# Putting every engine of an attention-plus-MLP kernel into hand-made program order, with a pipelined start and more PSUM banks for the first MLP group

## The chip, the cores and the metric

The kernel runs on one core of a Trainium2 chip. The metric is device time in microseconds of one launch, lower is better; beside it the text uses the span of one profiled launch. A launch takes 1.8 us more than its own span; the medians quoted are of other launches too. With one core there is no second die to compare; every run quoted here is of the fast state (within 1.5% of the fastest of its kernel), and every experiment is on record as correct.

Engine names in the profile: PE does matmuls, PEld loads their weights, DVE is the vector engine, ACT the scalar engine, POOL the GpSimd engine, SP issues most DMAs. SBUF is the on-chip memory; PSUM is the accumulator memory that PE writes; this kernel uses it as 8 banks, each of 128 partitions by 512 float32.

## The reference, cut to what matters

Two stages. First a causal linear attention with a decay per head, in blocks of 64 tokens with a carried state, then an MLP on the result (B=4, H=8, S=768, D=64; 3072 tokens, 512 to 2048 to 512):

```python
for b in range(nb):                      # blocks of 64 tokens, in order
    intra = einsum('bhic,bhjc->bhij', qb, kb) * Dmask
    intra = einsum('bhij,bhjd->bhid', intra, vb)
    inter = einsum('bhid,bhde->bhie', qb * lam_pow, kv_state)
    out[:, :, sl] = intra + inter
    kv_state = lam_block * kv_state + einsum('bhsd,bhse->bhde', kb * rev_pow, vb)
...
h = x @ w_in
s = sin(alpha * h)
g = h + s * s / (alpha + 1e-09)
return g @ w_out
```

## The kernel before

The attention is cut into 24 units (one batch, half of the heads, 256 tokens). Four units make a group of 512 tokens, which the MLP then takes. A unit goes through: scale q and k (into QL and KD) and cast v (into VB), eight transposes into PSUM, a copy of them to SBUF (QT), the score matmuls, a mask (ST), the output matmuls, and an update of the state. The MLP of a group has 16 blocks of `ffn1` (four matmuls of 128x512 into one PSUM bank, then sine on ACT, square on DVE or POOL, and `gall` on DVE, which reads the bank once more), and four tiles of `ffn2` (16 matmuls each, a copy to `ob` on ACT, a store).

The parts that matter (cuts marked with `...`):

```python
    RING = 10
    GATE = 9
    ...
    work = ctx.enter_context(tc.tile_pool(name="work", bufs=3))
    xtp = ctx.enter_context(tc.tile_pool(name="xt", bufs=3))
    outp = ctx.enter_context(tc.tile_pool(name="outp", bufs=3))     # ob
    ps = ctx.enter_context(tc.tile_pool(name="ps", bufs=1, space=PS))
    ...
    def transposes(u):                       # PSUM tag "s": one tile of two banks
        pt = ps.tile([P, 2, 2, 2, P], BF16, name="pt", tag="s", bufs=1)
        ...
    def scores(u):
        sp = ps.tile([P, 2, 2, 2, P], FP32, name="sp", tag="s", bufs=1)   # two banks
        ...                                  # 16 matmuls, then the mask in two halves
        for hd in range(2):
            nc.vector.tensor_tensor(out=ST[:, hd], in0=sp[:, hd], in1=mask..., op=ALU.mult)
    ...
    def ffn1(g, f, sq=None):
        hps = ps.tile([P, 512], FP32, name="hps", tag="hps", bufs=3)      # one bank
        ...                                  # 4 matmuls into hps
        def fin():
            nc.scalar.activation(out=s1[:], in_=hps[:], func=ACTF.Sin, scale=alpha_sb[:, f:f + 1])
            (sq or nc.vector).tensor_tensor(out=s2[:], in0=s1[:], in1=s1[:], op=ALU.mult)
            nc.vector.scalar_tensor_tensor(out=gall[g][:, f, :], in0=s2[:],
                                           scalar=r_sb[:, f:f + 1], in1=hps[:],
                                           op0=ALU.mult, op1=ALU.add)
        ...
    def ffn2(g, m):
        ops = ps.tile([P, DM], FP32, name="ops", tag="ops", bufs=1)
        ...                                  # 16 matmuls
        def fin():
            ob = outp.tile([P, DM], FP32, name="ob")
            nc.scalar.copy(out=ob[:], in_=ops[:])
            ...
            nc.sync.dma_start(out=out[r0:r0 + C, :].rearrange("(p two) d -> two p d", two=2),
                              in_=ob[:])
    ...
    with tc.manual_schedule(engines={ET.PE, ET.Pool, ET.SP}):
        ...                                  # units 0 to 3 one after the other
        for f in range(NFC):                 # first MLP group
            run(ffn1(0, f, nc.gpsimd if f % 2 else nc.vector))
            if f == GATE:                    # loads of units 4 to 13 wait for this block
                load(4, after=f1mm[0, f])
                for u in range(5, 4 + RING):
                    load(u)
        ...                                  # slots 4 to 27: a unit, and blocks of ffn1 and
                                             # ffn2 of earlier groups in between; ffn2(0) is
                                             # spread over slots 4 to 11
        for i in range(4):
            run(ffn2(NG - 1, i))             # the tail
```

PE, POOL and SP take their instructions in the order in which the program writes them; the order on ACT and DVE is left to the scheduler. The gate is the block of the first MLP group (`GATE`) whose last matmul releases the 30 loads of units 4 to 13. The eight PSUM banks are: the two-bank tile `s`, the two-bank tile `okv`, three `hps`, one `ops`. Each load or store is 256 KB.

## Time and profile before

The median is 268.04 us (2 runs, 267.77 to 268.31); the profiled launch has a span of 265.8 us.

| stage | from to, us | limit |
|---|---|---|
| first four units | 0 to 32.8 | latency chain, PE 11.15 busy of 32.80 |
| first MLP group | 32.8 to 54.8 | one bank after the other comes free, PE 16.28 of 22.00 |
| units 4 to 7 | 54.8 to 78.2 | inputs landing, and POOL (18.99 of 23.40) |
| units 8 to 11 | 78.2 to 108.3 | about 7.5 us a slot, PE 24.86 of 30.10 |
| steady slots | 108.3 to 253.5 | PE, 141.52 of 145.20; 8.37 us a slot |
| last stores | 253.5 to 265.8 | DMA, no engine busy |

The table is read from the windows view: for each stretch its length, then the busy time of each engine (with the count of instructions), the granted PE clock (1.00 is full), the busy share of the 16 DMA engines, and GB/s. The boundaries are the events of the profile: the first `ffn1` matmul, the last `gall` of the first MLP group, the scores of unit 8 and of unit 12, and the end of the last copy into `ob`. Before:

```profile
core 0: us, PE busy (x) PEld busy (x) DVE busy (x) ACT busy (x) POOL busy (x), PEclk, DMA share, GB/s
0.00:32.80 32.80, 11.15 (x233) 8.42 (x235) 13.17 (x38) 9.91 (x14) 18.82 (x39) 1.00 0.79 161
32.80:54.80 22.00, 16.28 (x62) 6.22 (x62) 14.91 (x24) 11.32 (x17) 11.77 (x13) 1.00 1.02 204
54.80:78.20 23.40, 18.83 (x269) 10.74 (x272) 7.11 (x16) 8.28 (x11) 18.99 (x30) 0.85 1.17 287
78.20:108.30 30.10, 24.86 (x322) 13.33 (x328) 21.99 (x45) 16.50 (x25) 18.09 (x28) 0.94 0.66 191
108.30:253.50 145.20, 141.52 (x1225) 71.87 (x1240) 99.50 (x172) 73.76 (x109) 44.85 (x59) 1.00 0.15 48
253.50:265.80 12.30, 0.00 (x0) 0.00 (x0) 0.00 (x0) 0.00 (x0) 0.00 (x0) 0.62 0.11 44
```

More than half of the span is bounded by PE and can't be shortened by a new order. What a new order can win lies in the first 108 us and at the end.

In the first stage the copy QT(0), which the first scores need, stands behind two casts that wait for DMA. ACT's timeline of the kernel before (start, duration, engine, line, what, and in brackets the idle time before it and what ended it):

```profile
9.62 0.62 ACT L174 CAST VB<-st_v 128x512 bf16<-128x512 f32 x1 [2.27 <-DMA st_v<-in_v_dram]
12.34 0.62 ACT L174 CAST VB<-st_v 128x512 bf16<-128x512 f32 x1 [2.10 <-DMA st_v<-in_v_dram]
12.86 1.00 ACT L196 COPY QT<-pt 128x1024 bf16<-128x1024 bf16 x1
```

In the first MLP group PE waits for DVE, since a bank is free only after its `gall`. The waits are short, 0.3 to 1.0 us after every one to four blocks. PE's timeline of the kernel before:

```profile
38.31 2.75 PE L334 MATMUL hps<-xt,w_in_sb 128*128 128x512 bf16 x12 [0.95 <-DVE gall L345]
42.93 4.26 PE L334 MATMUL hps<-xt,w_in_sb 128*128 128x512 bf16 x16 [0.56 <-DVE gall L345]
```

### The profile page before, as it was taken

The numbers are of one execution on the slowest core, as the hardware profiler recorded it, in microseconds if no ns is written. First come the engines' busy times: TensorE is split into PE (matmuls) and PEld (weight loads), VectorE is DVE, ScalarE is ACT, GpSimd is POOL, SyncE is SP. The second block draws the span as 40 slices with busy tenths as digits, with TensorE's granted clock in tenths as the row PEclk, the third lists the DMA queues.
The fourth block names the chain that finished last, engine by engine and source line by source line (L and its number), as shares of the span: only waits on it lengthen the run. The fifth ranks groups of instructions, "written<-read, shape, count | busy, mean of one in ns | idle before, by whom it ended". The sixth has DMA issues, their size and how long they took to land.

```text
span 265.8 us, 5296 instructions
## 1 busy us (share of the span) xinstructions
PE 212.6 (80%) x2104; PEld 110.6 (42%) x2129; DVE 156.7 (59%) x294; ACT 119.8 (45%) x174; POOL 112.5 (42%) x166
## 2 busy tenths in 40 slices
PE   0255488749969778899999999999999999997800
PEld 0144333224544444455455554555545444443300
DVE  3453357742345777796768778888778666660000
ACT  2343245513354566366545665456654544531000
POOL 4359664486894666644576455423500000000000
PEclk9999999968998999999999999999999999999975
DMA  6909999999984469733110001110011011111110
GB/s 164 295 20 146 172 155 166 281 292 292 291 243 149 123 186 286 217 114 107 41 36 26 31 32 42 30 31 29 35 39 31 30 35 38 39 38 50 51 51 39
DMA packets 45560, 29.71 MB, mean 112 GB/s; under 512 B 1488, under 2 KB 42464, under 8 KB 45536
## 3 DMA queue, kind: packets, MB, share of 16 engines
q1 hardware_dynamic: 41280, 25.17, 34.2%
q0 software_dynamic: 4224, 4.19, 10.0%
q8 instruction: 16, 0.26, 0.4%
q14 instruction: 8, 0.07, 0.1%
q10 hardware_dynamic: 32, 0.01, 0.0%
HBM read 27.28 MB, written 6.29 MB: 126 GB/s over the span
## 4 chain that ended last, share of the span: by engine, by line
PE 63%; POOL 13%; issue 6%; DVE 5%; ACT 4%; SPq 2%; DMA 2%; POOLq 0%; ACTq 0%
PE ops L356 30%; PE hps L334 24%; PE sp L211 3%; POOL KD L169 3%; PE pt L190 3%; POOL QL L166 2%; DMA st_v<-in_v_dram 2%; DVE gall L345 2%; SPq L74 2%; ACT QT L196 2%; PE okv L292 2%; PE okv L276 1%; POOL w_in_sb L145 1%; DVE ST L218 1%; DVE kvx L255 1%
## 5 line engine op out<-in xcount | busy, mean ns | idle before, releaser
L334 PE MATMUL hps<-xt,w_in_sb 128*128 128x512 bf16 x381 | 98.6, 384 | 7.8 <-DVE gall L345 6.8
L356 PE MATMUL ops<-w_out_sb,gall 128*128 128x512 bf16 x362 | 95.8, 387 | 4.0 <-ACT ob L363 2.1
L334 PEld LDWEIGHTS <-w_in_sb 128*128 128x128 bf16 x384 | 37.3, 99 | 53.3 <-issue 14.8
L356 PEld LDWEIGHTS <-gall 128*128 128x128 bf16 x384 | 36.3, 99 | 44.9 <-issue 5.6
L218 DVE TENSOR_TENSOR ST<-sp,mask 128x512 bf16<-128x512 f32 x48 | 32.1, 684 | 16.8 <-PE sp L211 16.8
L196 ACT COPY QT<-pt 128x1024 bf16<-128x1024 bf16 x24 | 24.3, 1011 | 26.7 <-PE pt L190 26.7
L169 POOL TENSOR_TENSOR KD<-st_k,R 128x512 bf16<-128x512 f32 x24 | 25.4, 1060 | 1.3 <-DVE R L126 0.8
L166 POOL TENSOR_TENSOR QL<-st_q,E 128x512 bf16<-128x512 f32 x20 | 22.4, 1122 | 0.0
L190 PE MATMUL pt<-iden,QL 128*128 128x128 bf16 x96 | 10.4, 238 | 14.2 <-DVE QL L166 7.4
L363 ACT COPY ob<-ops 128x512 f32<-128x512 f32 x24 | 14.1, 586 | 16.6 <-PE ops L356 15.2
L303 ACT CAST xt<-okv 128x512 bf16<-128x512 f32 x24 | 14.0, 585 | 14.0 <-PE okv L235 11.2
L211 PE MATMUL sp<-QT 64*64 64x128 bf16 x384 | 11.2, 241 | 6.4 <-ACT QT L196 6.1
L190 PEld LDWEIGHTS <-QL 128*128 128x128 bf16 x96 | 7.3, 104 | 19.8 <-DVE QL L166 7.4
L176 POOL CAST VB<-st_v 128x512 bf16<-128x512 f32 x20 | 13.1, 656 | 0.0
L190 PE MATMUL pt<-iden,KD 128*128 128x128 bf16 x96 | 10.5, 239 | 0.7 <-POOL KD L169 0.7
L211 PEld LDWEIGHTS <-QT 64*64 64x64 bf16 x384 | 6.9, 116 | 9.6 <-ACT QT L196 7.6
L292 PE MATMUL okv<-ST,VB 64*64 64x128 bf16 x384 | 10.5, 232 | 0.0
L235 PE MATMUL okv<-VB,KD 64*64 64x64 bf16 x320 | 7.7, 205 | 0.0
L292 PEld LDWEIGHTS <-VB 64*64 64x64 bf16 x384 | 7.6, 117 | 0.3 <-issue 0.2
L190 PEld LDWEIGHTS <-KD 128*128 128x128 bf16 x96 | 7.1, 107 | 1.2 <-POOL KD L169 1.2
L174 ACT CAST VB<-st_v 128x512 bf16<-128x512 f32 x4 | 2.5, 617 | 9.4 <-DMA st_v<-in_v_dram 9.4
L235 PEld LDWEIGHTS <-KD 64*64 64x64 bf16 x320 | 6.4, 122 | 0.0
(503 smaller groups left out, 278.2 us busy)
## 6 DMA issues: line engine op xcount, KB each, us to landing
st_q<-in_q_dram SPq DMA_DIRECT2D x24, 256.0 KB
st_k<-in_k_dram SPq DMA_DIRECT2D x24, 256.0 KB
st_v<-in_v_dram SPq DMA_DIRECT2D x24, 256.0 KB
out_dram<-ob SPq DMA_DIRECT2D x24, 256.0 KB
w_in_sb<-in_moe_w_in_dram POOLq DMA_DIRECT2D x4, 512.0 KB, 6.6
w_out_sb<-in_moe_w_out_dram POOLq DMA_DIRECT2D x4, 512.0 KB, 8.9
alpha_r<-in_moe_alpha_dram ACTq DMA_DIRECT2D x1, 8.0 KB
lam_bc<-in_lam_dram SPq DMA_DIRECT2D x1, 4.0 KB
```

The lines of the kernel that those rows point to most:

```text
L166: eq.tensor_tensor(out=QL[:], in0=qs[:].rearrange("p h two e -> p two h e"), in1=E[:, :, hs].unsqueeze(3).to_broadcast([P, 2, HH, D]), op= ...
L169: nc.gpsimd.tensor_tensor(out=KD[:], in0=ks[:].rearrange("p h two e -> p two h e"), in1=R[:, :, hs].unsqueeze(3).to_broadcast([P, 2, HH, D ...
L190: nc.tensor.transpose(out=pt[:, j, hp, par, :], in_=src[:, par, 2 * hp:2 * hp + 2, :], identity=iden[:])
L196: nc.scalar.copy(out=QT[:], in_=pt[:])
L211: nc.tensor.matmul(out=sp[half[c], hd, par, hp, :], lhsT=QT[half[hd], 1, hp, par, half[c]], rhs=QT[half[hd], 0, hp, :, half[c]], start=Tru ...
L218: nc.vector.tensor_tensor(out=ST[:, hd], in0=sp[:, hd], in1=mask[:].unsqueeze(2).to_broadcast([P, 2, 2, P]), op=ALU.mult)
L235: nc.tensor.matmul(out=okv[half[hd], c, 2 * P + hp * D:2 * P + (hp + 1) * D], lhsT=KD[half[c], par, h, :], rhs=VB[half[c], par, h, :], sta ...
L292: nc.tensor.matmul(out=okv[half[hd], c, hp * P:(hp + 1) * P], lhsT=VB[half[c], par, 2 * hp + hd, :], rhs=ST[half[c], hd, par, hp, :], star ...
L303: nc.scalar.copy(out=xt[g][:, 2 * hh:2 * hh + 2, bb, :, :].rearrange("p hp c i -> p c hp i"), in_=okv[:, :, 0:2 * P].rearrange("p c (hp i) ...
L334: f1mm[g, f] = nc.tensor.matmul(out=hps[:], lhsT=w_in_sb[:, c, f * P:(f + 1) * P], rhs=xt[g][:, c].rearrange("p b c i -> p (b c i)"), star ...
L356: nc.tensor.matmul(out=ops[:], lhsT=gall[g][:, f, m * P:(m + 1) * P], rhs=w_out_sb[:, f, :], start=(f == 0), stop=(f == NFC - 1))
L363: nc.scalar.copy(out=ob[:], in_=ops[:])
```

## The change

Its intent: put all engines into program order, so that nothing stands before what is needed next. The first four units are pipelined, each with its transposes one unit ahead and in `hps` banks, so that they don't share the bank pair of the scores. The first MLP group uses seven of the eight banks, so that PE is not held by three. `ffn2(0)` runs at once after the first MLP group instead of being spread over slots 4 to 11. The loads of units 4 to 13 go out after block 14 instead of 9. For units 4 to 9 the scaling of q moves from POOL to DVE, and the cast of v from POOL to ACT. The tail's `ffn2` alternates between two banks.

The core of the diff (cuts marked with `...`; the moved but unchanged bodies of the helpers are left out):

```diff
-    GATE = 9
+    GATE = 14
+    ctx.enter_context(tc.manual_schedule())
...
+    BUFS = {"s": 1, "okv": 1, "hps": 3, "ops": 1}
...
-    def transposes(u):
-        pt = ps.tile([P, 2, 2, 2, P], BF16, name="pt", tag="s", bufs=1)
+    def transposes(u, tag="s"):
+        pt = ps.tile([P, 2, 2, 2, P], BF16, name="pt", tag=tag, bufs=BUFS[tag])
...
+        if prev is None:
+            nc.scalar.copy(out=X[:], in_=A)          # was on the vector engine
...
-    def ffn1(g, f, sq=None):
+    def ffn1(g, f, sq=None, hps=None):
-        hps = ps.tile([P, 512], FP32, name="hps", tag="hps", bufs=3)
+        if hps is None:
+            hps = ps.tile([P, 512], FP32, name="hps", tag="hps", bufs=3)[:]
...
-    def ffn2(g, m):
-        ops = ps.tile([P, DM], FP32, name="ops", tag="ops", bufs=1)
+    def ffn2(g, m, tag="ops"):
+        ops = ps.tile([P, DM], FP32, name="ops", tag=tag, bufs=BUFS[tag])
...
+    for n in range(4):
+        if n < 3:
+            scale_q(n + 1, V), scale_k(n + 1, G), cast_v(n + 1, A)
+            transposes(n + 1, "hps")
+        ...                                          # unit n
+        if n == 1:
+            for j in range(4):
+                load_w_in(j)
...
-        for f in range(NFC):
-            run(ffn1(0, f, nc.gpsimd if f % 2 else nc.vector))
+    for tag in ("hps", "hps", "hps", "s", "okv", "hps", "hps", "hps", "s", "okv", "hps", "hps"):
+        if tag == "hps":
+            banks = [None]
+        else:
+            t2 = ps.tile([P, 2, 512], FP32, name="t2", tag=tag, bufs=1)
+            banks = [t2[:, 0, :], t2[:, 1, :]]
+        for bk in banks:
+            run(ffn1(0, f, G if f % 2 else V, bk))
             if f == GATE:
                 load(4, after=f1mm[0, f])
...
+    run(ffn2(0, 0))
+    run(ffn2(0, 1, "hps"))
+    F2 = blocks(ffn2(0, 2), 4) + blocks(ffn2(0, 3, "hps"), 4)
...                                                  # its last quarters stand in slot 4
+            if j == 1 and n + 1 < NU:                # slots 8 on; before: transposes later in the slot
+                transposes(n + 1)
...
-            run(ffn2(NG - 1, i))
+        run(ffn2(NG - 1, i, "hps" if i % 2 else "ops"))
```

## The prediction

> **What bounds it now.** Four regions, read from the timeline and the windows view.
> (a) 0 to 32.4 us: the first four attention units, a latency chain: PE is busy 10.2 of 30 us. ACT copies QT(0) only at 12.86, though its transposes ended at 8.9, because two v casts that wait for DMA stand before it.
> (b) 32.4 to 54.7: the first MLP group, 1.36 us a block of 512 columns against 0.86 of matmul; PE waits for gall (three banks).
> (c) 57.7 (scores of unit 4) to 108.25 (scores of unit 12): latency again; unit 8 starts at 78.2, then 7.4 to 7.8 us a slot with about 5.9 of PE.
> (d) 108 to 253.5: PE-bound, 8.37 us a slot, PE busy 8.35. In the tail three idles of 0.67 us wait for the one output bank. The last 12 us are output DMA.
>
> **What the change does, by region.**
> (a) QT(0) follows its transposes: scores(0) near 10.4 instead of 13.9. Most is lost again: all four w_in issues (0.8 us each on POOL) stand before unit 3's KD, whose transposes now precede scores(2), and each unit's transposes queue ahead of its predecessor's update. I expect the MLP to start at 31.3: gain 1 us.
> (b) Seven banks let PE run ahead; DVE then bounds a pair of blocks (0.46+0.75+0.75=1.96 us). Last gall near 50.8 instead of 54.75: another 3 us. The gate moves to block 14, so the loads of units 4 to 13 start near 45.6, as before (45.1).
> (c) ffn2(0) now runs at once, in three tiles and then a fourth inside unit 4. Scores(4) near 58.5, unit 5 near 63. Here is the trap: the order listing shows SP issuing all 30 loads before the first output store, and the fourth output copy (ob has three buffers) waiting on ACT for that store. Before, the 30th load was issued 25.3 us after the gate and the fourth copy came only at 102.6, after its buffer was long free. So the first store goes out near 71.8 and lands near 75; ACT, now in strict order, stands from about 63 until then, and with it outev(4), kvx(5), QT(6). From there, with traced durations, three half-finished units cost about 11.6 us: scores(8) near 87 (8.8 later than before). PE will be cold there: the Trainium skill ("TensorE: Matmul & The Clock Gate", Part 1) says an idle window halves the clock; this trace agrees (0.43 us between matmuls at 58.5 to 61.9, 0.216 later).
> Units 8 to 11 are bounded by DVE (6.55 us a slot plus a 0.5 stall behind mask, transposes, QT copy, sine): about 27.6 us instead of 30.05. Scores(12) near 114.5, +6.3.
> (d) Still PE-bound at 8.37; gain 0. Tail alternates banks: -2.0.
>
> Sum: -4 by the end of the first MLP, eaten by the ACT wait; +6.3 at unit 12, -2.0 in the tail: about +4. **Predicted 271.8 us, 80% range 266.5 to 276.5; chances: faster 0.06, same 0.60, slower 0.34.**
>
> **What would show it.** Right: an ACT idle of about 12 us before an ob copy at 63 to 75, released by a DMA; PE slices near 0 to 2 there; unit-8 scores near 87; first MLP about 19 us; tail idles gone; slots from 12 on at 8.37. Wrong: no ACT wait on a store; unit 8 before 78.
>
> **What would make it wrong.** Stores landing sooner than 3 us after issue, or loads issued faster than 0.87 us each (then near 262 if there were no wait at all); w_in landing late because all four are issued together; in-order ACT or DVE stalling PE in the long PE-bound region (0.2 us a slot would add 3).

## More of the kernel before

The DMA view of 253 to 266 us shows one DMA line at about 0.1 of the engines and a flat 50 GB/s until the end, where the middle of the run moves up to 292 GB/s:

```profile
GB/s 50 50 50 50 50 50 50 50 50 50 57 50 57 50 50 50 50 50 50 50 50 50 50 50 50 50 50 57 50 50 57 50 50 50 6 0 0 0 0 0
```

## The result, and the profile after

The kernel after takes 299.63 us (2 runs, 298.78 to 300.49) against 268.04. Ratios in this document are the mean time of one kernel's fast runs over the mean time of the other's in the same rounds, so not quite the ratio of the medians quoted. Here the ratio is 1.118 [1.103, 1.132]: nearly 12% slower, where about 1.4% slower was predicted, and outside the predicted range.

The windows view of the kernel after, cut at the same events as before:

```profile
0.00:31.80 31.80, 11.02 (x233) 8.39 (x235) 12.59 (x34) 10.50 (x18) 19.53 (x39) 1.00 0.80 166
31.80:65.10 33.30, 21.71 (x76) 8.69 (x77) 14.98 (x25) 11.32 (x17) 11.24 (x12) 0.85 0.47 83
65.10:107.50 42.40, 19.67 (x278) 11.62 (x281) 9.99 (x18) 12.68 (x22) 13.56 (x20) 0.70 0.77 202
107.50:138.10 30.60, 22.57 (x300) 12.56 (x304) 23.76 (x43) 14.92 (x23) 18.02 (x28) 0.92 0.84 224
138.10:282.00 143.90, 141.26 (x1226) 71.86 (x1240) 99.77 (x174) 74.15 (x110) 43.43 (x58) 1.00 0.12 38
282.00:297.00 15.00, 0.00 (x0) 0.00 (x0) 0.00 (x0) 0.01 (x1) 0.00 (x0) 0.65 0.12 45
```

Stage by stage against the kernel before: 1.0 us won in the first stage; 11.3 us lost in the first MLP group (33.3 against 22.0); 19.0 us lost in units 4 to 7 (42.4 against 23.4); 0.5 lost in units 8 to 11; 1.3 won in the steady slots and the tail's matmuls; 2.7 lost in the last stores. The two large losses are the subject of what follows.

**The first MLP group.** PE's timeline of the kernel after, in that stage:

```profile
35.20 1.03 PE L337 MATMUL t_547<-xt,w_in_sb 128*128 128x512 bf16 x4
39.20 1.02 PE L337 MATMUL t_547<-xt,w_in_sb 128*128 128x512 bf16 x4 [2.97 <-DVE gall L348]
...
43.82 1.62 PE L337 MATMUL t_566<-xt,w_in_sb 128*128 128x512 bf16 x4 [2.74 <-DVE gall L348]
...
53.08 1.02 PE L337 MATMUL t_615<-xt,w_in_sb 128*128 128x512 bf16 x4 [3.09 <-DVE gall L348]
...
58.01 1.86 PE L337 MATMUL t_634<-xt,w_in_sb 128*128 128x512 bf16 x4 [2.57 <-DVE gall L348]
```

Four times the second block of a two-bank tile (`t2`, here t_547, t_566, t_615 and t_634) waits for the `gall` of the first block of the same tile, although it writes the other bank: 2.97 + 2.74 + 3.09 + 2.57 = 11.4 us. Compare the waits of the kernel before, at most 0.95. The listing of the compiled instructions shows the same wait, on the first matmul of the second block (row 499; DVE_49 is a semaphore of the vector engine), and it could have been read before the prediction. Only the waits of ACT and SP had been read there. The listing names the other side: that matmul waits for the 40th count of DVE's semaphore, which is the `gall` of the first half of t_547, and the first matmuls of the other three second halves wait in the same way:

```
490 L337 Ldweights w_in_sb
491 L337 Matmult t_547<-xt,w_in_sb 128x512
...
498 L337 Ldweights w_in_sb [waits DMASW1_49]
499 L337 Matmult t_547<-xt,w_in_sb 128x512 [waits DVE_49]
```

**The output copy.** ACT's timeline and SP's queue of the kernel after (SPq lines are DMA issues):

```profile
75.90 1.01 ACT L198 COPY QT<-pt 128x1024 bf16<-128x1024 bf16 x1 [1.45 <-PE pt L195]
96.38 0.59 ACT L366 COPY ob<-ops 128x512 f32<-128x512 f32 x1 [19.47 <-DMA out_dram<-ob]
96.86 0.59 ACT L318 CAST xt<-okv 128x512 bf16<-128x512 f32 x1
```

```profile
61.47 0.37 SPq L77 DMA_DIRECT2D st_q<-in_q_dram  x1
...
86.60 0.78 SPq L77 DMA_DIRECT2D st_v<-in_v_dram  x1
87.47 10.53 SPq L369 DMA_DIRECT2D out_dram<-ob  x4
```

The fourth copy into `ob` needs the buffer of the first, whose store stands on SP behind all 30 gated loads. It waits 19.47 us, and in program order everything later on ACT waits with it. This is the trap that the prediction named, but it is longer (12 us were predicted) and it starts later, because the gate opens at 61.47 and not near 45.6.

The predicted cold PE is there too: the page's slices show the granted clock at 0.5 from about 82 to 111 us. This agrees with the Trainium skill, "TensorE: Matmul & The Clock Gate", Part 1, as used in the prediction. Two lines of the page of the kernel after, 40 slices of 7.4 us, in tenths:

```profile
PE   0534737499600578667899999999999999999800
PEclk9999998689955559999999999999999999999975
```

**Units 8 to 11.** PE's timeline after, once in each slot:

```profile
127.79 0.38 PE L195 MATMUL pt<-iden,QL 128*128 128x128 bf16 x4 [1.39 <-DVE ST L223]
```

The transposes use the same two-bank tile `s` as the scores, and wait for both masks. The slots take 7.25 to 7.85 us (7.05 was estimated). The next slot, unit 12's, the first of the steady ones, still has 1.04 us of this wait and takes 9.58 us.

**What did come.** The first copy QT(0) now starts at 9.09 (before 12.86), and the scores of unit 0 at 10.61 (10.4 predicted, 13.92 before). The steady slots after that of unit 12 are 8.38 us, as before.

### The profile page after: what moved, and what is told of

Same layout as the page of the kernel before. It is cut to its first block, busy times and chain, and to the rows that moved or that the text cites. A ratio compares the mean times of both kernels' runs of the same rounds, so it can differ in the third digit from the quotient of the medians.

```text
span 297.0 us, 5258 instructions
## 1 busy us (share of the span) xinstructions
PE 216.2 (73%) x2105; PEld 113.1 (38%) x2129; DVE 161.1 (54%) x292; ACT 123.6 (42%) x188; POOL 105.8 (36%) x154
## 4 chain that ended last, share of the span: by engine, by line
PE 51%; issue 11%; DVE 8%; POOL 3%; ACT 2%; DMA 2%; SPq 1%; ACTq 0%; POOLq 0%
PE ops L359 23%; PE hps L337 20%; PE pt L195 3%; DVE gall L348 3%; DVE ST L223 3%; DMA st_k<-in_k_dram 2%; PE sp L212 2%; PE okv L307 1%; PE okv L291 1%; ACT QT L198 1%; POOL KD L173 1%; SPq L77 1%; PE t_634 L337 1%; PE okv L240 1%; POOL s_612 L347 0%
## 5 line engine op out<-in xcount | busy, mean ns | idle before, releaser
L337 PE MATMUL hps<-xt,w_in_sb 128*128 128x512 bf16 x346 | 92.4, 394 | 4.3 <-DVE gall L348 3.4
L359 PE MATMUL ops<-w_out_sb,gall 128*128 128x512 bf16 x367 | 92.9, 379 | 0.9 <-issue 0.2
L337 PEld LDWEIGHTS <-w_in_sb 128*128 128x128 bf16 x384 | 38.7, 102 | 64.0 <-issue 24.9
L223 DVE TENSOR_TENSOR ST<-sp,mask 128x512 bf16<-128x512 f32 x48 | 30.8, 684 | 24.7 <-PE sp L212 24.7
L173 POOL TENSOR_TENSOR KD<-st_k,R 128x512 bf16<-128x512 f32 x24 | 26.8, 1115 | 6.6 <-DMA st_k<-in_k_dram 4.5
L318 ACT CAST xt<-okv 128x512 bf16<-128x512 f32 x24 | 14.1, 586 | 12.5 <-PE okv L240 10.4
L195 PEld LDWEIGHTS <-QL 128*128 128x128 bf16 x96 | 7.5, 108 | 21.5 <-DVE QL L164 8.0
L164 POOL TENSOR_TENSOR QL<-st_q,E 128x512 bf16<-128x512 f32 x14 | 15.6, 1117 | 0.0
L212 PE MATMUL sp<-QT 64*64 64x128 bf16 x384 | 11.6, 248 | 0.6 <-ACT QT L198 0.6
L307 PE MATMUL okv<-ST,VB 64*64 64x128 bf16 x384 | 11.2, 244 | 0.0
L182 ACT CAST VB<-st_v 128x512 bf16<-128x512 f32 x10 | 6.2, 625 | 11.5 <-DMA st_v<-in_v_dram 11.5
L184 POOL CAST VB<-st_v 128x512 bf16<-128x512 f32 x14 | 9.3, 662 | 0.0
L164 DVE TENSOR_TENSOR QL<-st_q,E 128x512 bf16<-128x512 f32 x10 | 7.3, 732 | 2.9 <-DMA st_q<-in_q_dram 2.8
```

The source lines that it names most:

```text
L164: eng.tensor_tensor(out=QL[:], in0=stage[u][0][:].rearrange("p h two e -> p two h e"), in1=E[:, :, hs].unsqueeze(3).to_broadcast([P, 2, HH ...
L173: eng.tensor_tensor(out=KD[:], in0=stage[u][1][:].rearrange("p h two e -> p two h e"), in1=R[:, :, hs].unsqueeze(3).to_broadcast([P, 2, HH ...
L184: eng.tensor_copy(out=VB[:], in_=v_in)
L195: nc.tensor.transpose(out=pt[:, j, hp, par, :], in_=cast[u, key][:, par, 2 * hp:2 * hp + 2, :], identity=iden[:])
L212: nc.tensor.matmul(out=sp[half[c], hd, par, hp, :], lhsT=QT[half[hd], 1, hp, par, half[c]], rhs=QT[half[hd], 0, hp, :, half[c]], start=Tru ...
L307: nc.tensor.matmul(out=okv[half[hd], c, hp * P:(hp + 1) * P], lhsT=VB[half[c], par, 2 * hp + hd, :], rhs=ST[half[c], hd, par, hp, :], star ...
```

## The experiments

Twelve kernels ran. All outputs are right. Theory A: the two blocks that share a two-bank tile are ordered as one, and this wait, not the number of banks, sets the first MLP group; the late gate and the wait for the store follow from it. Rival B: strict program order on ACT and DVE is what holds the MLP. For the second loss, theory C: the fourth output copy waits for the first store, which stands behind 30 loads. For the tail, theory D: the end is set by the queue of the last stores and not by the last matmuls.

All events below are of single profiles; the times are medians, and the ratio is to the kernel before in the same rounds. Some kernels have `xt` with two buffers instead of three; this only pays for the SBUF of a fourth `ob` buffer and was not tried alone.

| kernel | time, us | ratio to before [95%] | last gall of 1st MLP | scores(8) | scores(12) | last copy | span |
|---|---|---|---|---|---|---|---|
| before | 268.04 | 1 | 54.75 | 78.2 | 108.25 | 253.48 | 265.8 |
| after | 299.63 | 1.118 [1.103, 1.132] | 65.05 | 107.45 | 138.13 | 282.02 | 297.0 |
| e1_pairs | 285.35 | 1.062 [1.059, 1.066] | 59.56 | 94.65 | 126.27 | 268.97 | 283.7 |
| e2_ob4 | 281.65 | 1.049 [1.043, 1.054] | 66.6 | 91.02 | 122.8 | 265.49 | 280.5 |
| e3_spread | 283.93 | 1.057 [1.052, 1.063] | 64.93 | 103.31 | 134.31 | 278.21 | 282.6 |
| e4_pairs_ob4 | 275.0 | 1.024 [1.016, 1.032] | 57.92 | 82.82 | 113.64 | 257.54 | 272.3 |
| e5_before_spread | 259.51 | 0.969 [0.965, 0.973] | 55.37 | 79.35 | 108.44 | 253.68 | 257.8 |
| e6_before_tail | 268.14 | 1.001 [0.997, 1.005] | 55.09 | 78.64 | 108.67 | 251.36 | 266.1 |
| e8_hps3 | 286.62 | 1.070 [1.064, 1.076] | 53.59 | 95.09 | 125.17 | 269.05 | 284.1 |
| e12_split_ob4 | 264.07 | 0.986 [0.981, 0.990] | 52.55 | 75.66 | 104.68 | 247.38 | 262.4 |
| e15_split_ob4_spread | 254.15 | 0.949 [0.946, 0.953] | 52.95 | 76.05 | 105.17 | 247.87 | 252.3 |
| e16_plus_j2 | 253.85 | 0.948 [0.943, 0.954] | 53.52 | 78.22 | 105.48 | 248.18 | 252.6 |
| e13_best | 249.96 | 0.934 [0.930, 0.938] | 49.88 | 72.99 | 100.26 | 242.95 | 247.4 |
| e17_squares_dve | 251.09 | 0.938 [0.933, 0.942] | 49.92 | 74.88 | 102.07 | 244.77 | 248.9 |

The kernel before measured 268.51, 267.94, 267.29 and 267.78 us in the four calls, so a difference of two ratios times 268 is used below where kernels of different calls are compared.

### e1_pairs: both blocks of a pair multiplied before either is used

```diff
-        for bk in banks:
-            run(ffn1(0, f, G if f % 2 else V, bk))
+        bl = [ffn1(0, f + i, G if (f + i) % 2 else V, bk) for i, bk in enumerate(banks)]
+        for s_ in bl:
+            run(s_[:-1])                 # the matmuls of both banks
+        for s_ in bl:
+            run(s_[-1:])                 # sine, square, gall
```

> The changed kernel, with one edit in the first MLP group: where two blocks of 512 columns share a two-bank tile, both blocks' matmuls are emitted before either block's sine, square and gall. Theory A (the second block's matmul waits for the first block's gall because both halves are one tile; four such pairs cost about 3 us each and cool the clock): the four PE waits of 2.6 to 3.1 us before t vanish, the first MLP takes about 20 us instead of 32, the gated loads start near 46 instead of 61.5, the ACT wait for the store stays and ends about 35 us after the gate (81 instead of 96.4), total about 284 us. Rival B (strict program order on DVE, where each odd block's gall stands behind the square on POOL, is what stretches it): the first MLP stays above 28 us, total above 294 us.

Measured 285.35 us, 14 us less than after. The last `gall` of the first MLP group came at 59.56 instead of 65.05, the first gated load at 49.04 instead of 61.47, and ACT's wait for the store was 10.29 us instead of 19.47. PE's waits in the pairs shrank to 0.33 and 1.31 us. So the wait between the two halves is a cause, and it does push the gate and the store. But the group still took 28.3 us where theory A had 20, just inside what rival B had foretold (above 28), while the total is what theory A had foretold. e1 alone does not decide between the two. Something besides PE's wait was left; e4 shows it, and e8 tests rival B.

### e2_ob4: a fourth output buffer

```diff
-    xtp = ctx.enter_context(tc.tile_pool(name="xt", bufs=3))
+    xtp = ctx.enter_context(tc.tile_pool(name="xt", bufs=2))
-    outp = ctx.enter_context(tc.tile_pool(name="outp", bufs=3))
+    outp = ctx.enter_context(tc.tile_pool(name="outp", bufs=4))
```

> The changed kernel with four output staging buffers instead of three (paid for by two xt buffers instead of three). Theory A (ACT in program order stands at the fourth output copy until the first store has landed, and everything behind it waits): the 19.5 us ACT wait is gone, total about 281 us. Rival (the wait only covers for something else that is as late, the gated input loads of units 6 to 9): ACT or POOL waits for input loads instead, and less than 6 us is gained, total above 293 us.

Measured 281.65 us, 18 us less than after. The first MLP group is as slow as in after (last `gall` at 66.6), SP still issues its first gated load only at 62.19, and yet ACT has no wait for a store any more: the fourth copy starts at 79.35 after 0.71 us of waiting for PE. The scores of unit 8 came 16.4 us earlier. ACT's timeline of e2:

```profile
79.35 0.58 ACT L366 COPY ob<-ops 128x512 f32<-128x512 f32 x1 [0.71 <-PE ops L359]
```

Theory C holds, with its size.

### e3_spread: each store cut in two by token parity

The store's outer dimension has two elements. The edit issues one store for each, of 64 partitions:

```diff
-            nc.sync.dma_start(out=out[r0:r0 + C, :].rearrange("(p two) d -> two p d", two=2),
-                              in_=ob[:])
+            ov = out[r0:r0 + C, :].rearrange("(p two) d -> two p d", two=2)
+            for t in range(2):
+                nc.sync.dma_start(out=ov[t], in_=ob[t * D:(t + 1) * D, :])
```

> The changed kernel with each output store issued as two stores of 64 partitions (rows of one parity each) instead of one with an outer dimension of two. Theory A (a store with an outer dimension of two runs on two of 16 DMA engines, 51 GB/s, 5.1 us each, so that stores queue at the end): a store lands about 3 us after issue, the ACT wait ends near 90.5 instead of 96.4, and the time from the last output copy to the end of the span falls from 15.0 to about 4 us; total about 282 us. Rival (the time after a store is a fixed completion latency or memory write speed): store rate stays near 51 GB/s, the end stays above 12 us, total above 296 us.

Measured 283.93 us. The span after the last copy fell from 15.0 to 4.4 us. ACT's wait for the store got shorter by 4.05 us; the copy now starts 5.0 us after the issue of the first store (87.26) and not 8.9. ACT's timeline of e3:

```profile
92.22 0.59 ACT L366 COPY ob<-ops 128x512 f32<-128x512 f32 x1 [15.42 <-DMA out_dram<-ob]
```

So a store of the old form is slow to land. The DMA packets of the two traces divide the time (a store's packets have 2048 bytes, a load's 512). In after, the first store's packets run from 90.2 to 95.7 us: 2.7 us before the first, 5.5 of transfer, 0.7 until the copy. In e3 the first 128 store packets, as many bytes, run from 89.5 to 90.7: 2.2 us, 1.2 and 1.5. Loads were still moving when the stores began (load packets until 91.2 us in after). With no load beside it, at the end of e5, the first packet moves 1.1 us after the issue. So an estimated 1.1 to 1.6 us of the wait are due to the loads; no run tested that alone.

### e4_pairs_ob4: e1 and e2 together

> The changed kernel with both the pair order of the first run and the fourth output buffer of the second. Theory A (two independent stalls, one after the other): the gains add, about 15 and about 15 us (the store wait would be some 15 us long with the earlier gate), total about 269 us. If the two overlap, the total is above 276 us.

Measured 275.0 us where 269 was expected, a miss. With both losses thought to be removed the kernel was still 2.4% slower than before. The trace shows where: the sine of the second block waits for the first block's `gall` as well, although sine and `gall` read different banks. ACT's timeline of e4 in the first MLP group:

```profile
49.24 1.27 ACT L344 ACTIVATE s<-t,alpha_sb 128x512 bf16<-128x512 f32 x2 [3.44 <-DVE gall L348]
53.18 0.69 ACT L344 ACTIVATE s<-t,alpha_sb 128x512 bf16<-128x512 f32 x1 [2.67 <-DVE gall L348]
```

So e1 had moved only the matmuls out of each other's way. The readers of the two halves are ordered too. The mended theory A: everything that touches the two-bank tile is ordered as if it touched one thing, and only separate tiles can show what seven banks are worth.

### e8_hps3: after, with three banks in the first MLP group

```diff
-    for tag in ("hps", "hps", "hps", "s", "okv", "hps", "hps", "hps", "s", "okv", "hps", "hps"):
+    for tag in ("hps",) * NFC:
```

> The changed kernel with the first MLP group on the three one-bank tiles alone, in the same program order on every engine. Theory A (tiles of two banks shared by two blocks cause the stretch): the first MLP takes 21 to 24 us instead of 32.5, although it has four banks fewer; the gate opens near 51, the ACT store wait ends 35 us later, total about 289 us. Rival B (program order on DVE causes the stretch): the first MLP takes at least 31 us, total at least 298 us.

Measured 286.62 us. This keeps the program order of all engines and takes the shared tiles away. The group ran from 31.33 to 53.59, 22.3 us, as in the kernel before (21.9), with PE waits of the old size. PE's timeline of e8:

```profile
37.01 4.16 PE L337 MATMUL hps<-xt,w_in_sb 128*128 128x512 bf16 x16 [0.75 <-DVE gall L348]
41.83 4.21 PE L337 MATMUL hps<-xt,w_in_sb 128*128 128x512 bf16 x16 [0.66 <-DVE gall L348]
```

So program order costs at most 0.4 us in this group, and rival B falls. The rest of the loss is the wait for the store, which this kernel keeps (18.50 us).

### e12_split_ob4: one tile for each bank, and the fourth output buffer

The two-bank tile `s` becomes two one-bank tiles, for the scores and for the MLP; `okv` gives one bank, and `ops` makes the seventh:

```diff
-    BUFS = {"s": 1, "okv": 1, "hps": 3, "ops": 1}
+    BUFS = {"s": 2, "okv": 1, "hps": 3, "ops": 1}
-        sp = ps.tile([P, 2, 2, 2, P], FP32, name="sp", tag="s", bufs=1)
+        sp = [ps.tile([P, 2, 2, P], FP32, name="sp", tag="s", bufs=2) for _ in range(2)]
-                            out=sp[half[c], hd, par, hp, :],
+                            out=sp[hd][half[c], par, hp, :],
-                out=ST[:, hd], in0=sp[:, hd],
+                out=ST[:, hd], in0=sp[hd][:],
-    for tag in ("hps", "hps", "hps", "s", "okv", "hps", "hps", "hps", "s", "okv", "hps", "hps"):
+    for tag in ("hps",) * 3 + ("s", "s", "okv", "ops") + ("hps",) * 3 + ("s", "s", "okv") + ("hps",) * 3:
...                                      # each a tile of one bank; okv: its first half only
```

> The changed kernel with four output buffers, and the first MLP group on seven one-bank tiles that no two blocks share (the two-bank score tile becomes two one-bank tiles). The pair-order run with four buffers measured 275.0 us where 269 was expected; its trace shows the second block's sine on ACT waiting for the first block's gall in each shared tile (3.4 and 2.7 us at the end). Theory A extended (every access to a shared tile is put in order, by matmul and by sine): no such ACT or PE wait, last gall near 51 instead of 57.9, first MLP about 20 us, total about 268.5 us. Rival (program order on DVE holds the rest): last gall after 55, total above 272 us.

Measured 264.07 us, 1.5% faster than before (1.0 to 1.9%, clear of the noise), and 4.4 us less than expected. PE's timeline of e12 in the first MLP group shows 14 blocks with no named wait and one of 0.59 us before the last two (its `t` tiles are the borrowed banks):

```profile
34.88 3.62 PE L337 MATMUL t<-xt,w_in_sb 128*128 128x512 bf16 x16
38.33 2.75 PE L337 MATMUL hps<-xt,w_in_sb 128*128 128x512 bf16 x12
40.92 2.75 PE L337 MATMUL t<-xt,w_in_sb 128*128 128x512 bf16 x12
43.52 1.02 PE L337 MATMUL hps<-xt,w_in_sb 128*128 128x512 bf16 x4
45.14 1.89 PE L337 MATMUL hps<-xt,w_in_sb 128*128 128x512 bf16 x8 [0.59 <-DVE gall L348]
```

The clock in this stage is 1.00 again (0.85 in after). But DVE still ends at 52.55, only 1.0 us before e8 with its three banks (31.20 to 52.55 is 21.35 us, against 22.26). So seven banks do let PE run ahead, as intended, but once they are separate tiles they are worth 1 us: DVE is the limit then, busy 16.16 of the 17.55 us from 35.00 on.

The split also takes units 8 to 11 from 30.68 us to 29.02: the slots of units 10 and 11 fall from 7.85 to 6.92 us, and the wait of the transposes for the mask from 1.39 to 0.76. The slot of unit 12 falls from 9.58 to 8.38.

The Trainium skill, "PSUM — Partial Sum Buffer", section "PSUM bank collisions raise a hardware error", says that a collision needs the same bank and the same quadrant of partitions, and that accesses of two engines to different banks run clean. By that the waits between the two halves of `t2` protected nothing. This agrees so far as it goes: e12 has no such waits and is correct. The listings agree too. In e4's the sine of each second half waits for the `gall` of the first half of its tile; in e12's each first matmul of a block that waits for a `gall` waits for that of the earlier block in its own bank. That the framework which makes the instructions tracks a tile as one object is inferred from this; its own bookkeeping was not looked into.

### e5_before_spread and e6_before_tail: the end of the kernel, on the kernel before

e5 is the kernel before with the stores of e3. e6 is the kernel before with the alternating tail alone:

```diff
-            run(ffn2(NG - 1, i))
+            run(ffn2(NG - 1, i, "hps" if i % 2 else "ops"))
```

> The kernel before, with each output store issued as two stores of 64 partitions, nothing else. Theory A (two of 16 DMA engines carry a store at 51 GB/s, and the last five stores queue): the time from the last output copy to the end falls from 12.3 to about 3.5 us, total about 259.5 us against 268.3. Rival (the end is completion latency or the speed of the memory): total within 1.5 us of the kernel before.

> The kernel before, with only the tail of the change: the last four output tiles alternate between two accumulation banks. Theory A (the end is set by the queue of the last five stores, each 5.1 us, counted from the issue of the fifth-last, which the tail does not move): PE and the last copy end 2.0 us earlier, the time after the last copy grows from 12.3 to about 14.3 us, total unchanged within 0.5 us. Rival (the prediction on record: minus 2.0 us in the tail): total about 266.2 us.

e5: 259.51 us, 3.1% faster than before by this edit alone. e6: 268.14 us, no change. In e6 the last copy came at 251.36 instead of 253.48, and the wait after it grew from 12.3 to 14.7 us. From the issue of the fifth-last store to the end of the kernel it is 29.6 us in before (236.2 to 265.8), 29.4 in e6 (236.7 to 266.1) and 29.7 in after (267.3 to 297.0), whatever the matmuls do in between. Theory D holds. The windows view of e6 and then of e5, from about the fifth-last store and from the last copies on:

```profile
236.00:252.00 16.00, 14.69 (x69) 6.47 (x66) 2.25 (x4) 3.62 (x6) 0.00 (x0) 1.00 0.13 46
252.00:266.10 14.10, 0.00 (x0) 0.00 (x0) 0.00 (x0) 0.00 (x0) 0.00 (x0) 0.55 0.12 45
```

```profile
236.00:253.70 17.70, 14.94 (x68) 6.35 (x65) 2.03 (x4) 3.44 (x6) 0.00 (x0) 1.00 0.27 60
253.70:257.80 4.10, 0.00 (x0) 0.00 (x0) 0.00 (x0) 0.00 (x0) 0.00 (x0) 1.00 0.29 64
```

In e6 the DMA share is 0.13 while the stores run: two of 16 engines busy. The steady rate is 50 to 51 GB/s, so that 262144 bytes take 5.1 us, longer than the 4.3 us between two copies. The stores queue up, and the queue ends the kernel. The Trainium skill, "DMA: Bandwidth & Descriptors", section "Why a DMA increments its semaphore by 16 and not by 1", says that the engine count is the largest number up to 16 that divides the slowest dimensions of both sides. With an outer dimension of two that is two engines, as the trace shows. With 64 partitions outermost the DMA view of e5 moves up to 246 GB/s, and a half store lands in 2.3 us:

```profile
GB/s 0 0 0 0 0 0 0 0 0 0 0 0 0 0 115 229 180 213 229 164 197 229 213 246 66 17 0 0 0 0 0 0 0 0 0 0 0 0 0 0
out_dram<-ob SPq DMA_DIRECT2D x2, 128.0 KB, 2.3
```

### e15, e16, e13: towards a version that beats both

e15 is e12 with the stores of e3. e16 adds to it that the transposes of slots from 8 on come one block later. e13 adds to that the four `w_in` loads two by two, earlier:

```diff
 # e16
-            if j == 1 and n + 1 < NU:
+            if j == 2 and n + 1 < NU:
                 transposes(n + 1)
 # e13
             scale_q(n + 1, V), scale_k(n + 1, G), cast_v(n + 1, A)
+            if n < 2:
+                load_w_in(2 * n)
+                load_w_in(2 * n + 1)
             transposes(n + 1, "hps")
...
-        if n == 1:
-            for j in range(4):
-                load_w_in(j)
```

> The run with seven unshared one-bank tiles and four output buffers (264.1 us), with each store also issued as two stores of 64 partitions. If the store queue is all that stands after the last output copy, the end shrinks from about 15 to about 4 us: total about 253.5 us. If something else at the end or a new contention with the loads takes it back, above 257 us.

> The run before this one, with the transposes of the next unit moved one block later in each slot (after the third block of the first MLP instead of the second). Theory (in the slots of units 8 to 11 the transposes wait for the mask on DVE, the QT copy waits for them, and the second sine stands behind that copy on ACT, so DVE idles 0.9 us in each slot of 7.85 us and PE waits 1.4): the slots take about 6.7 us, four of them gain about 4.5 us, total about 249 us. Rival (DVE work alone sets the slot): within 1.5 us of the run before this one.

> The run before this one, with the four weight loads of POOL issued two by two behind the KD scaling of units 1 and 2 instead of four in a row before that of unit 3. Theory (POOL's 3.2 us of issuing stand before KD of unit 3, its transposes and the scores of unit 2): scores of unit 2 come about 3 us earlier, and so does all that follows, total about 246 us. Rival (the weights then compete with the input loads of units 2 and 3 and delay them by as much): within 1 us of the run before this one.

e15 took 254.15 us. The stores are worth 3.6% of 268, 9.7 us, on top of e12, more than in e5, because e12 also ends its matmuls sooner and had waited longer (15.0 us).

e16 took 253.85 us (252.67 to 255.48), no different from e15; 249 was expected, and by the total alone the rival would stand. Its slots 8 and 9 did fall from 7.65 and 7.63 us to 6.65 and 6.77, so unit 12 should have come 1.9 us earlier, but unit 8 came 2.2 us later in its profile (78.22 against 76.05). 0.6 us of that are there at the last `gall`; the other 1.6 us are in one group of `ffn2` matmuls that the edit does not touch, with the same wait before it. PE's timeline of e15, then of e16:

```profile
53.00 4.71 PE L359 MATMUL ops<-w_out_sb,gall 128*128 128x512 bf16 x21 [0.27 <-DVE gall L348]
```

```profile
53.57 6.30 PE L359 MATMUL ops<-w_out_sb,gall 128*128 128x512 bf16 x21 [0.27 <-DVE gall L348]
```

The granted clock of these 5 us is 1.00 in e15 and 0.67 in e16. So the slots gained (all four take 27.3 us, against 29.1 in e15) and a colder clock took it back, in this profile. Why the clock differs, and how often it does, was not settled.

e13 took 249.96 us: 6.6% faster than before, and 3.9 us faster than e16 (the 246 expected had counted on the 4.5 us of e16 that did not come). The scores of unit 2 start at 20.95 instead of 24.02, and everything after follows. So the four loads in a row, 3.19 us on POOL at 18.74 in the kernel after, had stood in front of KD(3), as the prediction said.

### e17_squares_dve: all squares of the first MLP group on DVE

In the kernel after, and in all before this one, every second square of the first group is on POOL. e17 is e13 with all 16 on DVE.

```diff
-            run(ffn1(0, f, G if f % 2 else V, bk))
+            run(ffn1(0, f, V, bk))
```

> The fastest version so far, with all squares of the first MLP group on DVE instead of every other one on POOL. Theory (a square on DVE takes 0.91 instead of 0.42 us when a square runs on POOL at the same time): all sixteen squares take about 0.43 us on DVE; a pair of blocks takes 2.4 us of DVE instead of 2.27, so the first MLP is about 1 us longer and the total about 1 us more, 251 us. Rival (something else, such as the many banks in flight, slows DVE's square): squares of 0.9 us remain, and the first MLP gets some 5 us longer.

Measured 251.09 us, 1.1 us more than e13 (ratio 0.938 against 0.934; the intervals overlap, so even the sign is not certain). The question was why a pair of blocks takes DVE 2.27 us in e13 where 1.96 had been estimated. DVE's timeline of e13, then POOL's, then DVE's of e17:

```profile
42.97 0.92 DVE L347 TENSOR_TENSOR s<-s 128x512 bf16<-128x512 bf16 x1
```

```profile
42.57 1.04 POOL L347 TENSOR_TENSOR s<-s 128x512 bf16<-128x512 bf16 x1 [1.24 <-DVE gall L348]
```

```profile
43.04 0.42 DVE L347 TENSOR_TENSOR s<-s 128x512 bf16<-128x512 bf16 x1
```

The same square takes DVE 0.42 us alone and 0.92 us beside POOL's. With all squares on DVE a pair costs it 2.24 us (four lines of its timeline, 40.80 to 43.04), so moving half of them to POOL saves it nothing: the last `gall` of the group comes at 49.88 in e13 and at 49.92 in e17 (21.8 and 21.5 us after the group's first matmul). What e17 lost in its profile it lost after that, in the same group of 21 `ffn2` matmuls as e16 (6.39 us in place of 4.71, clock 0.66), so the 1.1 us say little about the squares. The Trainium skill, "SBUF — State Buffer", section "Who interferes with whom", has DVE and GpSimd share a port pair under an exclusive lock, which a DVE instruction with two inputs in SBUF, as the square, contends for with a GpSimd instruction that reads SBUF. The times fit that: DVE's square started 0.40 us after POOL's and finished 0.28 us after it.

## Why the prediction failed, point by point

1. **Region (a), right.** The scores of unit 0 at 10.61 (10.4 predicted), the MLP at 31.81 (31.3). The first reason given for the lost gain, the four `w_in` issues, was confirmed by e13; the second, the order of the transposes, was not tested.

2. **Region (b), the step that failed: "Seven banks let PE run ahead; DVE then bounds a pair of blocks (0.46+0.75+0.75=1.96 us). Last gall near 50.8 instead of 54.75."** Measured 65.05. Two of each pair of banks were one tile, and its two halves were ordered one after the other: PE waited 11.4 us in four waits, ACT's sine waited as well (e4), and the clock fell to 0.85. With separate tiles (e12) the group ended at 52.55. The bound of 1.96 us per pair was too low as well: it took DVE's square alone for granted, and beside POOL's square it takes 0.92 us and not 0.46, so that a pair costs 2.27 us. Even without the shared tile the gain was about 1 us over three banks (e12 against e8), not 3.

3. **"The loads of units 4 to 13 start near 45.6, as before": a consequence.** They started at 61.47, since block 14's matmul came that late. In e8 the gate opened at 49.82.

4. **Region (c), mechanism right, one size off.** The first store went out 26.0 us after the gate (26.2 predicted). But "lands near 75", 3.2 us after its issue, was wrong: the copy that waited for it started 8.9 us after the issue. The store uses two DMA engines, and its bytes take 5.1 us there with nothing beside them, which the last 12 us of the profile before had shown as 50 GB/s. From the end of ACT's wait to the scores of unit 8 it took 11.1 us (11.6 predicted). So unit 8's 20.4 us (107.45 against 87) are 15.9 of late gate, 5.7 of late landing, and about -1.1 in the two other terms. e2 confirms the whole: without the wait 18 us vanish.

5. **Units 8 to 11, too low by 3.1 us.** 30.68 against "about 27.6". A stall of 0.5 us was put down for the chain of mask, transposes, copy and sine; the transposes alone waited 1.39 us for both halves of the mask, since they too share the two-bank tile. It is the same oversight as in point 2, and e12 shows what it cost: with separate tiles the four slots take 29.02 us, 1.7 less. With the transposes one block later too they take 27.3 (e16), so the rest of the 3.1 was the place of the transposes in the slot.

6. **Region (d), right but for one slot, and "Tail alternates banks: -2.0", wrong.** The steady slots are 8.38 us, except that of unit 12 with 9.58. The last copy did come earlier against the same work (in e6 142.7 us after scores(12), before 145.2), but the end is set by the queue of stores; the gain was 0 (e6), and the last stores grew from 12.3 to 15.0 us.

The sum closes. Against the predicted 271.8 the measured time is 27.8 us more: 20.4 until unit 8, 3.1 in units 8 to 11, 0.7 in the steady slots and the tail's matmuls (143.9 where 145.2 - 2.0 = 143.2 was expected: 1.2 lost in unit 12's slot, 0.5 more won in the tail), 2.7 in the last stores: 26.9. The rest is 0.4 us more between the profiled span and the median (2.6 against 2.2), and rounding in the prediction's own sum.

The prediction's own list of what could make it wrong had "stores landing sooner" and "in-order ACT or DVE stalling PE in the long PE-bound region". Neither came. What came was an assumption that was never on the list: that a bank given to a block is a bank free of its neighbour.

What stays open: why the clock after the first MLP group is 1.00 in some profiles and about 0.66 in others (e16, e17), which hides what the later transposes are worth; what `xt` with two buffers costs; whether block 14 is the best place for the gate. Cutting each store in two doubles the number of store issues (24 to 48), which did no harm here.

## What to carry to other kernels

Give each PSUM bank that is used on its own a tile of its own; two blocks in one two-bank tile wait for each other, and the compiled listing shows it if the waits of every engine are read, not only those of the engines that one suspects. In strict program order, look at each copy that needs a buffer back from a store: everything behind it on that engine waits too, so give it a buffer more, or let the store go out before the loads. And look at the rate of the last DMAs first: where the end is a queue of stores at 50 GB/s, an earlier last matmul wins nothing, and a store with a longer outer dimension was worth 3.1% alone.

## What the Trainium skill lacked or had wrong

- "PSUM — Partial Sum Buffer" tells which accesses collide, but no page says that a tile of two banks is ordered as one by the program that is built from it. Here that cost four PE waits of 2.57 to 3.09 us, further waits of ACT (3.44 and 2.67 us in e4), 0.9 us in each of the slots of units 10 and 11, and 1.2 in that of unit 12.
- "DMA: Bandwidth & Descriptors" has the rule for the number of engines and the advice to put a dimension of a multiple of 16 outermost, but no measured cost of leaving it out, above all at the end of a kernel: stores with an outer dimension of two ran at 50 to 51 GB/s, 5.1 us each, and five of them in a queue set the end (29.6 and 29.7 us from the issue of the fifth-last). Its figure of about 27 GiB/s per engine (29 GB/s) was not reached: 51 GB/s over two engines are 25.5 GB/s each.
- "TensorE: Matmul & The Clock Gate", section "Back-to-back issue gap", gives about 131 ns for a sustained stream of 512-column matmuls with weight loads. In this kernel's PE-bound slots four such matmuls take 0.86 us, 215 ns each, at full clock. This is the value that the section gives for an isolated matmul (about 216 ns) and calls too high for a stream.
- "SBUF — State Buffer", section "Who interferes with whom": it held, and gives no example of the cost of splitting equal work between the two engines. Here a DVE square took 0.42 us alone and 0.92 us beside POOL's, so that half of the squares on POOL moved the end of the group by 0.04 us (49.88 against 49.92), and the group was no shorter for it (21.8 against 21.5 us).
